# Reordering the opening of a Mamba-2 block that feeds an MLP: where the long row sums, the weights' exponents and their signs are made

## The chip, the cores and the metric

The kernel runs on one core of a Trainium2 chip. The metric is the device time of one execution in microseconds (us). Several runs are taken, and their median counts. One further execution was recorded by the hardware profiler; views of the profile and the trace below are of that execution.

The engines are named as in the profile: PE is TensorE's matrix products, PEld its weight loads, DVE is VectorE, ACT is ScalarE, POOL is GpSimd and SP is SyncE, whose queue issues most of the transfers. A name like L579 is a line of the kernel before the change. The changed kernel's lines lie one to three later.

## The reference

Two parts follow each other. The first is a state-space block over 4 batches, 8 heads and 768 tokens, with head size 32 and state size 16; the second is an MLP over the 3072 tokens, with 256 features in, 2048 inside and 256 out.

```python
log_a = np.log(np.clip(a, 1e-06, 1.0))
for c in range(nc):                       # blocks of tokens
    cum = np.cumsum(la, axis=-1)
    L = np.exp(cum[..., :, None] - cum[..., None, :]) * causal
    M = einsum('bhin,bhjn->bhij', Cc, Bc) * L
    y = einsum('bhij,bhjd->bhid', M, xc) \
        + einsum('bhin,bhnd->bhid', Cc, state) * exp(cum)
    state = exp(sum(la)) * state \
        + sum_j(Bc * xc * exp(cum[..., -1:] - cum))
x = y.transpose(0, 2, 1, 3).reshape(3072, 256)
h = x @ w_in
out = (h * clip(h + 3, 0, 6) / 6) @ w_out
```

All inputs but `w_in` and `w_out` are float32; those two are float64 and come to the kernel as pairs of 32-bit words.

## The kernel before the change

**Blocks.** The 768 tokens of each batch are worked on in six blocks of 128 (halves of 64 inside the block); all four batches and eight heads of a block go together. Block 0 goes through the state-space part first. Then the MLP of block k runs on TensorE while the state-space part of block k + 1 and the preparation of block k + 2 are put between its products by hand. The order of the instructions on each engine is the order of the calls in the program; each engine works its own list in that order and waits by semaphores for the data.

**The opening.** All that the change touches is between the first transfer and the first product of block 0's MLP:

- SyncE issues the loads of `a`, of `C` for block 0 (eight transfers, L101), of `x` (L119) and of the second quarter of `w_in` (L139). ScalarE's queue issues the first quarter of `w_in` and block 0's `B`.
- `log_a` clips `a` and takes the logarithm (L264, L266). `add_up` makes running sums along a row with one VectorE scan (L269), in two pieces: the columns of blocks 0 and 1 (256 wide), and those of blocks 2 to 5 (512 wide). Only the first piece is needed for blocks 0 and 1.
- Blocks 0 and 1 get their decays from products: `diff_mask`, `mask_again`, `diff_less` and `diff_pick` write the differences of the sums into PSUM (L336, L343, L348, L357), and `diff_exp` takes the exponential on ScalarE (L365). Blocks 2 to 5 get theirs from memory: `store_rows` sends the long sums to DRAM (`cum_e`, `cum_d`, L286 and L288) to be loaded again, spread over the partitions; `turn_cum` turns them on TensorE into `c_ps` (L316), and `by_token` copies `c_ps`, negated, into `cum_n` (L319). `cum_n` is used as a bias from block 2 on.
- `turn_b` turns `B` on TensorE (L422) and copies it on ScalarE (L431). `turn_squares` (L465) and `part_heads` (L475) turn `C` on VectorE; `fade` (L481, GpSimd) scales it for the products with the state.
- `scores` forms the products of C and B on TensorE (L530) in four PSUM banks, f0 to f3, and then, in `into_state`, the new states (L548). `multiply` reads the states on ScalarE (L564, L574) and multiplies the scores into the decays on VectorE, one multiply for each of the four banks (L579).
- `mix` forms y from these and x (L625) and from the state (L503), in two halves of the heads; `keep` copies it to SBUF on ScalarE (L639). The first projection (`mlp_in`, L647) begins with that, in 16 units of 128 inner features.
- `busy(n, bank)` puts n idle products into a bank (L493): 128x512 in float32, whose results nobody reads.

**The weights.** A quarter of the float64 words is turned to float32 by `decode(i)`, a generator; each call of `weights(i, n)` runs n steps of it. Quarters 0 to 3 are `w_in`, 4 to 7 are `w_out`. Its steps: a copy of the top 16 bits (ScalarE, L198); the significand (VectorE, L201, L205); exponent and sign masked out (VectorE, L215, L217); the exponent in two steps on ScalarE (L221, L223); sign and exponent joined by a bitwise OR (VectorE, L228) and the product with the significand (VectorE, L236), these two in one step. Three raw buffers are in use, so `load_w` for quarter i + 3 waits until quarter i is read.

The PSUM tiles c_ps (bank f1) and the idle tile (bank f0) are allocated behind `multiply`, which reads the scores from these banks.

Of the kernel before, what the change touches and what calls it, by code (L numbers as in the profile page):

```python
# [8 lines left out]
FP32 = mybir.dt.float32  # L9
# [5 lines left out]
ALU = mybir.AluOpType  # L15
# [6 lines left out]
def kernel(  # L22
# [24 lines left out]
    nc = tc.nc  # L47
    P = 128
    NB, NH, S, D = x.shape
    N = B.shape[-1]  # L50
    DM, DF = moe_w_in.shape[0], moe_w_out.shape[0]
    NC = S // P
# [15 lines left out]
    ps = ctx.enter_context(tc.tile_pool(name="ps", bufs=1, space=PSUM))  # L68
# [7 lines left out]
    G = NB * NH  # L76
# [51 lines left out]
    def load_w(i, queue=nc.sync):  # L128

        raw = loads.tile([P, NK * FP * 2 * P], U32, name="raw", bufs=NRAW)  # L130
        if i < NP:
            cols = slice(2 * i * FP * P, 2 * (i + 1) * FP * P)
            src = moe_w_in[:, cols].rearrange("(k p) f -> p k f", p=P)
            dst = raw.rearrange("p (k f) -> p k f", k=NK)
        else:
            r0 = (i - NP) * FP * P
            src = moe_w_out[r0:r0 + FP * P, :].rearrange("(k p) m -> p k m", p=P)
            dst = raw.rearrange("p (k m) -> p k m", k=FP)
        queue.dma_start(out=dst, in_=src)  # L139
        raws[i] = raw  # L140
# [14 lines left out]
    def conceal_in(t, pattern):  # L155
# [24 lines left out]
        out=head, in_=head, pattern=[[-2 * N, NQ], [-N, 2]], compare_op=ALU.is_ge,  # L180
        fill=0.0, base=0, channel_multiplier=1)
    nc.gpsimd.affine_select(
        out=head, in_=head, pattern=[[2 * N, NQ], [N, 2]], compare_op=ALU.is_ge,
# [3 lines left out]
    def decode(i):  # L187

        n = NK * FP * P
        top = raws[i].bitcast(U16).rearrange("p (n w) -> p n w", w=4)[:, :, 3]
        lo, hi = (raws[i].rearrange("p (n w) -> p n w", w=2)[:, :, w] for w in range(2))
        s = att.tile([P, n], U16, name="ws")
        e = att.tile([P, n], U16, name="we")
        m = att.tile([P, n], U32, name="wm")
        nc.scalar.copy(out=s, in_=top)  # L198

        def significand():  # L200
            nc.vector.tensor_scalar(  # L201
                out=m, in0=hi, scalar1=0xFFFFF, scalar2=0x100000,
                op0=ALU.bitwise_and, op1=ALU.bitwise_or)
            yield
            nc.vector.scalar_tensor_tensor(  # L205
                out=m.bitcast(FP32), in0=lo, scalar=2.0 ** -32, in1=m, op0=ALU.mult,
                op1=ALU.add)
            yield

        parts_m = significand()  # L210
        if i == 0:
            next(parts_m)
            next(parts_m)
        yield
        nc.vector.tensor_scalar(  # L215
            out=e, in0=s, scalar1=0x7FF0, scalar2=None, op0=ALU.bitwise_and)
        nc.vector.tensor_scalar(  # L217
            out=s, in0=s, scalar1=0x8000, scalar2=None, op0=ALU.bitwise_and)
        next(parts_m, None)
        yield  # L220
        nc.scalar.activation(e.bitcast(BF16), e, AF.Relu, bias=bias_hi, scale=-8.0)  # L221
        yield
        nc.scalar.activation(e, e.bitcast(BF16), AF.Relu, bias=bias_lo, scale=-1.0)  # L223
        next(parts_m, None)
        if i and i + NRAW < 2 * NP:
            load_w(i + NRAW)
        yield
        nc.vector.tensor_tensor(out=e, in0=e, in1=s, op=ALU.bitwise_or)  # L228
        m, e = m.bitcast(FP32), e.bitcast(BF16)
        if i < NP:  # L230
            dst = w_in[i]
            m, e = (t.rearrange("p (k f) -> p k f", k=NK) for t in (m, e))
        else:
            dst = w_out[:, (i - NP) * FP:(i - NP + 1) * FP, :]
            m, e = (t.rearrange("p (k f) -> p k f", k=FP) for t in (m, e))
        nc.vector.scalar_tensor_tensor(  # L236
            out=dst, in0=m, scalar=2.0 ** -20, in1=e, op0=ALU.mult, op1=ALU.mult)
# [12 lines left out]
    ends_at = (slice(0, 2 * P), slice(2 * P, S))  # L250
# [17 lines left out]
    def add_up(sl):  # L268
        nc.vector.tensor_tensor_scan(  # L269
            out=cum[:, sl], data0=run.rearrange("g c p -> g (c p)")[:, sl], data1=a_sb[:, sl],  # L270
            initial=0.0, op0=ALU.mult, op1=ALU.add)
# [13 lines left out]
    def store_rows():  # L285
        nc.sync.dma_start(  # L286
            out=cum_e[1:].rearrange("c g p -> g c p"), in_=cum_c[:, 1:])
        nc.sync.dma_start(  # L288
            out=cum_d[2:].rearrange("c a g i -> g (c a) i"),
            in_=cum[:, 2 * P:].rearrange("g (k i) -> g k i", i=HT))  # L290
# [21 lines left out]
    cum_n = const.tile([P, NC, G], FP32, name="cum_n")  # L312

    def turn_cum(c_ps):
        for c in range(2, NC):
            nc.tensor.transpose(out=c_ps[:, c], in_=cum_c[:, c], identity=ident[:G, :G])  # L316

    def by_token(c_ps):
        nc.vector.tensor_scalar(  # L319
            out=cum_n[:, 2:], in0=c_ps[:, 2:], scalar1=-1.0, scalar2=None, op0=ALU.mult)  # L320


    yTs, states, mids, bTs, bss, tmps = {}, {}, {}, {}, {}, {}
# [67 lines left out]
    def ends(c, b):  # L391

        if b == 0:
            bss[c] = att.tile([P, G, N], FP32, name="bs", bufs=1)
        hs = slice(b * NH, b * NH + NH)
        nc.gpsimd.tensor_tensor(  # L396
            out=bss[c][:, hs], in0=Bs[c][:, hs],
            in1=Ls[c][:, b, :, HT - 1:HT].to_broadcast([P, NH, N]), op=ALU.mult)
# [8 lines left out]
    def turned(c):  # L407
        if c not in bTs:
            bTs[c] = [att.tile([P, NB, P], FP32, name="bT", bufs=1),
                      att.tile([P, NB, 2, P], FP32, name="cT", bufs=1),  # L410
                      att.tile([P, NB, P], FP32, name="csT", bufs=1)]
        return bTs[c]

    def turn_ps(c, j):

        if c < 2:
            return ps.tile([P, NB, P], FP32, name="t_ps", tag=f"f{2 * j if c else 1}")
        return ps_o.tile([P, NB, P], FP32, name="t_ps", tag="o")

    def transposes(c, j, t_ps):  # L420
        for b in range(NB):
            nc.tensor.transpose(  # L422
                out=t_ps[:, b],
                in_=bcs[c][j][:, b * NH:(b + 1) * NH].rearrange("s h n -> s (h n)"),
                identity=ident)

    def turn_b(c):

        t_ps = turn_ps(c, 1)
        transposes(c, 1, t_ps)  # L430
        nc.scalar.copy(out=turned(c)[0], in_=t_ps)  # L431
# [47 lines left out]
    def fade(c, sl=slice(0, P), engine=nc.vector):  # L479
        csT = turned(c)[2][:, :, sl]  # L480
        engine.tensor_tensor(out=csT, in0=csT, in1=etos[c][:, :, sl], op=ALU.mult)  # L481
# [8 lines left out]
    def busy(n, bank):  # L490

        for _ in range(n):
            nc.tensor.matmul(  # L493
                out=bank.rearrange("p (b i) -> p b i", b=NB), lhsT=ident,
                rhs=ident.unsqueeze(1).to_broadcast([P, NB, P]), start=True, stop=True)
# [117 lines left out]
    def mix(c):  # L613


        xt = xts[c]
        if (1, 0) not in ys[c]:
            own_halves(c)
        more = c in range(TURN, NC - 1)
        for u in range(2):  # L620
            for b in range(NB):
                for h in range(u * HU, (u + 1) * HU):
                    for a, rows in enumerate(HALF):
                        d0 = D * (h % HU)
                        nc.tensor.matmul(  # L625
                            out=ys[c][a, u][d0:d0 + D, b], lhsT=xt[rows, b * NH + h],
                            rhs=Ls[c][rows, b, h], start=(b == 0 and a >= min(c, 1) and u >= more), stop=True,
                            tile_position=(a * HT, d0), skip_group_check=True)
            if c == 0:
                from_state(c, 1, (2 * u, 2 * u + 1))  # L630
        if c:
            from_state(c, 1)
# [373 lines left out]


    parts = {i: decode(i) for i in range(2 * NP)}

    def weights(i, n):  # L1010
        for _ in range(n):
            next(parts[i], None)


    def diff(c, *bs):
        for part in (diff_less, diff_pick):
            for b in bs:
                part(c, b)
# [16 lines left out]
    first_eto()  # L1035
    diff(1, 2, 3)
    weights(0, 1)
    for b in range(NB):
        ends(0, b)
    turn_b(0)  # L1040
    diff(1, 0, 1)
    weights(0, 1)
    diff_exp(1, 2)
# [1 line left out]
    turn_squares(bcs[0][0], turned(0)[2])  # L1045
    part_heads(0)
    fade(0, HALF[1], nc.gpsimd)
    add_up(ends_at[1])
    store_rows()
    load_w(2)  # L1050
    weights(0, 1)
# [1 line left out]
    scores(0)  # L1053
    multiply(0)
    load_w(3)
    c_ps = ps.tile([P, NC, G], FP32, name="c_ps", tag="f1")
    turn_cum(c_ps)
    busy(1, ps.tile([P, NB * P], FP32, name="d", tag="f0"))
    weights(0, 1)
    weights(1, 1)  # L1060
    by_token(c_ps)
    mix(0)
    keep(0)
    weights(1, 3)
# [180 lines left out]
```

## Time and profile before

| what | value |
|---|---|
| median of 3 runs | 340.89 us (340.2 to 341.09) |
| the profiled execution | 339.78 us, span of its instructions 337.6 us |
| TensorE (PE) busy | 330.6 us |
| VectorE (DVE) busy | 234.5 us |
| ScalarE (ACT) busy | 199.4 us |
| GpSimd (POOL) busy | 123.9 us |
| data moved | 25.15 MB |
| first product of block 0's MLP (L647) | 22.53 us after the start of the span |

The profiled execution took 339.78 us; 2.2 us of that lie outside the span, which runs from the first to the last instruction in the trace. Times in the timeline count from the start of the span. A timeline row gives start, duration, engine, line, operation, what it writes and reads, and in brackets how long the engine was idle before it and what ended that. A row with "x2" or "x4" merges that many instructions, and its duration runs from the first start to the last end. In the chain of waits each row is a link of the chain that ended last: start, length, what. In busy times by stretch, each row is a stretch and the busy time in it of PE, PEld, DVE, ACT and POOL, then the clock that the throttle granted, the busy share of the 16 DMA engines and GB/s.

### The profile page before, as it was taken

What the parts mean: (1) busy time and instruction counts of PE and PEld (TensorE: products, weight loads), DVE (VectorE), ACT (ScalarE), POOL (GpSimd) and SP (SyncE); (2) the same over time, 40 slices, a digit from 0 to 9 for tenths busy, and PEclk for the clock granted to TensorE, in tenths of its full rate; (3) what the DMA queues carried; (4) which work ended last, traced back from release to release, by engine and by line L of the source; (5) the groups of instructions that cost most, each with busy time, mean ns of one, the idle gap of its engine ahead of it and who ended that gap; (6) DMA issues with size and microseconds to landing.
All of it is one profiled execution on the core that took longest, in us unless ns stands there. A gap on an engine that the chain in (4) does not pass through costs nothing.

```text
span 337.6 us, 8192 instructions
## 1 busy us (share of the span) xinstructions
PE 330.6 (98%) x3337; PEld 265.4 (79%) x3337; DVE 234.5 (69%) x380; ACT 199.4 (59%) x418; POOL 123.9 (37%) x123
## 2 busy tenths in 40 slices
PE   6999999999999999999999999999999999999996
PEld 2554448888888888888888888888888888899995
DVE  6699999998399739755339556355477355599974
ACT  4769878757986670576461576570486030577661
POOL 3300000290184799089813079911079800000000
PEclk9999999999999999999999999999999999999999
DMA  8999968042590215258107267101160001110001
GB/s 174 165 316 201 208 219 184 2 54 76 139 142 1 57 37 139 33 72 78 33 13 156 33 83 69 28 4 17 27 81 2 2 2 18 26 21 2 1 2 62
DMA packets 89605, 25.15 MB, mean 75 GB/s; under 512 B 82208, under 2 KB 85952, under 8 KB 89056
## 3 DMA queue, kind: packets, MB, share of 16 engines
q1 hardware_dynamic: 85184, 23.33, 37.5%
q10 hardware_dynamic: 4384, 1.31, 1.8%
q8 instruction: 26, 0.43, 0.5%
q14 instruction: 11, 0.09, 0.1%
HBM read 21.33 MB, written 3.29 MB: 73 GB/s over the span
## 4 chain that ended last, share of the span: by engine, by line
PE 94%; DMA 3%; DVE 1%; SPq 1%; issue 0%; DVEq 0%
PE h L715 33%; PE wb L914 13%; PE wc L914 8%; PE o L772 8%; PE h L647 8%; PE wa L914 8%; PE o_end L880 6%; PE y L625 3%; PE y L503 2%; PE cb L530 2%; DMA raw<-in_moe_w_in_dram 2%; DMA pairs<-in_C_dram 1%; PE y L548 1%; SPq L101 1%; PE o_end L898 1%; PE sp L548 0%
## 5 line engine op out<-in xcount | busy, mean ns | idle before, releaser
L759 DVE SCALAR_TENSOR_TENSOR gT<-gT,h 128x512 f32<-128x512 f32 x96 | 64.8, 684 | 33.8 <-ACT gT L754 32.2
L754 ACT ACTIVATE gT<-h,half 128x512 f32<-128x512 f32 x96 | 65.2, 685 | 25.6 <-PE h L715 23.6
L735 ACT ACTIVATE h<-h 128x512 f32<-128x512 f32 x66 | 38.2, 585 | 39.0 <-PE h L715 38.8
L715 PE MATMUL h<-y_hi,w_part 128*128 128x512 f32 x160 | 51.5, 407 | 0.0
L715 PE MATMUL h<-y_less,w_part 128*128 128x512 f32 x160 | 50.1, 399 | 0.0
L715 PE MATMUL h<-y_lo,w_part 128*128 128x512 f32 x160 | 49.5, 395 | 0.0
L818 POOL TENSOR_TENSOR s<-gT 128x512 f32<-128x512 f32 x16 | 23.8, 1490 | 46.7 <-DVE gT L759 46.7
L715 PEld LDWEIGHTS h<-y_lo,w_part 128*128 128x128 f32 x160 | 30.0, 188 | 7.3
L715 PEld LDWEIGHTS h<-y_hi,w_part 128*128 128x128 f32 x160 | 30.0, 188 | 6.8 <-DVE gT L759 0.2
L715 PEld LDWEIGHTS h<-y_less,w_part 128*128 128x128 f32 x160 | 29.2, 188 | 6.0 <-ACT h L735 0.2
L385 ACT ACTIVATE L<-L,cum_n 128x64 f32<-128x64 f32 x128 | 31.6, 336 | 0.0
L772 PE MATMUL o<-w_out,gT 128*128 128x256 f32 x128 | 28.8, 381 | 0.0
L647 PE MATMUL h<-yT,w_in 128*128 128x512 f32 x64 | 27.7, 594 | 0.0
L772 PEld LDWEIGHTS o<-w_out,gT 128*128 128x128 f32 x128 | 24.1, 190 | 3.8 <-issue 0.5
L647 PEld LDWEIGHTS h<-yT,w_in 128*128 128x128 f32 x64 | 12.1, 190 | 14.9 <-issue 13.2
L158 POOL TENSOR_SCALAR_AFFINE_SELECT L<-L 64x1024 f32<-64x1024 f32 (+1 forms) x16 | 20.4, 1281 | 8.5 <-DMA L<-cum_d 8.0
L579 DVE TENSOR_TENSOR L<-L,cb 128x512 f32<-128x512 f32 x24 | 15.0, 681 | 11.7 <-PE cb L530 11.7
L403 POOL TENSOR_TENSOR tmp<-state,eto 128x256 f32<-128x256 f32 x5 | 3.2, 643 | 52.8 <-ACT eto L389 48.9
L818 POOL TENSOR_TENSOR s<-gT,s 128x512 f32<-128x512 f32 x16 | 21.7, 1364 | 0.9
L396 POOL TENSOR_TENSOR bs<-B,L 128x128 f32<-128x128 f32 x24 | 11.2, 486 | 29.5 <-ACT L L385 20.9
L880 PE MATMUL o_end<-v_pair,g_pair 128*128 128x256 f32 x120 | 21.1, 281 | 0.0
L818 POOL TENSOR_TENSOR gT<-gT 128x512 f32<-128x512 f32 x16 | 20.4, 1279 | 0.9
(140 smaller groups left out, 593.0 us busy)
## 6 DMA issues: line engine op xcount, KB each, us to landing
raw<-in_moe_w_out_dram SPq DMA_DIRECT2D x4, 1024.0 KB
L<-cum_d SPq DMA_DIRECT2D x8, 512.0 KB
xt<-in_x_dram SPq DMA_DIRECT2D x6, 512.0 KB
raw<-in_moe_w_in_dram SPq DMA_DIRECT2D x3, 1024.0 KB
out_dram<-back SPq DMA_DIRECT2D x128, 16.0 KB
pairs<-in_C_dram SPq DMA_DIRECT2D x40, 32.0 KB
eto<-cum_e SPq DMA_DIRECT2D x20, 64.0 KB
B<-in_B_dram SPq DMA_DIRECT2D x5, 256.0 KB
```

Of the source, the lines that this page charges most:

```text
L158: nc.gpsimd.affine_select(out=t[rows], in_=t[rows], pattern=pattern, compare_op=ALU.is_ge, fill=-1e5, base=base, channel_multiplier=-1)
L385: nc.scalar.activation(Ls[c][:, b, h], Ls[c][:, b, h], AF.Exp, bias=cum_n[:, c, g:g + 1])
L579: nc.vector.tensor_tensor(out=Ls[c][:, :, hs], in0=Ls[c][:, :, hs], in1=cbs[c][q], op=ALU.mult)
L647: nc.tensor.matmul(out=h, lhsT=w_in[f // FP][:, j, f % FP * P:(f % FP + 1) * P], rhs=yTs[k][:, j].rearrange("p b i -> p (b i)"), start=(j ...
L715: nc.tensor.matmul(out=hs_[k, f], lhsT=w[j][:, f % FP * P:(f % FP + 1) * P], rhs=y[:, j], start=(start and j == 0), stop=True, skip_group_ ...
L735: nc.scalar.activation(h, h, AF.Copy, scale=1.0 / EPS + 1.0)
L754: nc.scalar.activation(gTs[k][:, f], h, AF.Relu, bias=half, scale=1.0 / 6.0)
L759: nc.vector.scalar_tensor_tensor(out=g, in0=g, scalar=1.0, in1=h, op0=ALU.min, op1=ALU.mult)
L772: nc.tensor.matmul(out=o[:, b % 2], lhsT=gTs[0][:, f, b * P:(b + 1) * P], rhs=w_out[:, f], start=(f == 0 and b % 2 == 0), stop=True, skip_ ...
L818: nc.gpsimd.tensor_tensor(out=o, in0=p_, in1=q_, op=op)
L880: nc.tensor.matmul(out=ends_["cross" if n == 2 else "squares"][b], lhsT=g_parts[t][n][:, b * P:(b + 1) * P], rhs=w, start=(t == 0 and b < ...
L914: nc.tensor.matmul(out=bank[:, slot], lhsT=lhs[:, j], rhs=rhs[:, j], start=(clear and j == 0), stop=True, skip_group_check=True)
```

## The change

Four edits, all in the opening:

1. The long piece of the row sums (`add_up(ends_at[1])`) is made ahead of C's turning on VectorE instead of behind it. With that, `turn_cum` and `by_token` move from behind `multiply` to right behind `turn_b`, `c_ps` takes bank f2 instead of f1, and `store_rows` finds its sums made earlier.
2. `by_token` runs on ScalarE instead of VectorE.
3. One step of `weights(0, 1)` is moved, so that the first exponent step (L221) comes ahead of the copy of the turned B on ScalarE. For quarter 0 `decode` gets one more `yield`, between the OR and the product: the OR runs ahead of `scores` and `multiply`, and the product stays behind them.
4. `busy(1)` ahead of `mix` is left out. `busy(2)` ahead of `scores` stays.

```diff
@@ decode
         yield
         nc.vector.tensor_tensor(out=e, in0=e, in1=s, op=ALU.bitwise_or)
+        if i == 0:
+            yield
         m, e = m.bitcast(FP32), e.bitcast(BF16)
@@ by_token
-        nc.vector.tensor_scalar(
-            out=cum_n[:, 2:], in0=c_ps[:, 2:], scalar1=-1.0, scalar2=None, op0=ALU.mult)
+        nc.scalar.mul(cum_n[:, 2:], c_ps[:, 2:], -1.0)
@@ the opening
     first_eto()
     diff(1, 2, 3)
     weights(0, 1)
+    add_up(ends_at[1])
     for b in range(NB):
         ends(0, b)
+    weights(0, 1)
     turn_b(0)
+    c_ps = ps.tile([P, NC, G], FP32, name="c_ps", tag="f2")
+    turn_cum(c_ps)
+    by_token(c_ps)
     diff(1, 0, 1)
     weights(0, 1)
     diff_exp(1, 2)
     diff_exp(1, 3)
     turn_squares(bcs[0][0], turned(0)[2])
     part_heads(0)
     fade(0, HALF[1], nc.gpsimd)
-    add_up(ends_at[1])
     store_rows()
     load_w(2)
     weights(0, 1)
     busy(2, ps.tile([P, NB * P], FP32, name="d", tag="f3"))
     scores(0)
     multiply(0)
     load_w(3)
-    c_ps = ps.tile([P, NC, G], FP32, name="c_ps", tag="f1")
-    turn_cum(c_ps)
-    busy(1, ps.tile([P, NB * P], FP32, name="d", tag="f0"))
     weights(0, 1)
     weights(1, 1)
-    by_token(c_ps)
     mix(0)
     keep(0)
```

## The prediction

> **What bounds the kernel now.** I read the page first, then the chain of waits from the start to 52 us, then the timeline of the first 24 us engine by engine, then busy time by stretches. From the page:
>
> ```profile
> PE 330.6 (98%) x3337; PEld 265.4 (79%) x3337; DVE 234.5 (69%) x380; ACT 199.4 (59%) x418; POOL 123.9 (37%) x123
> ...
> PE 94%; DMA 3%; DVE 1%; SPq 1%; issue 0%; DVEq 0%
> ```
>
> TensorE is 94% of the chain that ends last; only the opening has other links. The chain there (start us, us, what):
>
> ```profile
> 8.91 4.00 DMA pairs<-in_C_dram
> ...
> 13.09 1.17 DVE csT L465
> ...
> 14.28 0.89 DVE cT L475 x2
> ...
> 15.30 1.25 PE cb L530 x59
> ...
> 16.56 1.30 DVE L L579 x2
> ...
> 17.90 0.43 PE c_ps L316 x4
> 18.33 1.05 PE d L493 x2
> 19.39 1.00 PE y L625 x57
> 20.38 0.61 PE y L503 x16
> 20.99 1.00 PE y L625 x54
> 21.99 0.61 PE y L503 x16
> 22.60 27.66 PE h L647 x64
> ```
>
> The opening waits for C to land (12.91), turns it on VectorE, forms the scores, multiplies them into the decays, and after two of the four multiplies goes to TensorE and stays there. Between the second multiply (17.86) and the mixing (19.39) stand two things that the mixing doesn't use: the turning of the row sums (c_ps, needed only from block 2 on) and two idle passes of `busy(1)`. From 22.60 on TensorE has no gap; the stretch below (busy time of PE, PEld, DVE, ACT, POOL; clock; DMA) stands for those after it up to 330 us, so what the opening saves or loses reaches the end unless a producer falls behind.
>
> ```profile
> 14.60:16.40 1.80, 1.37 (x65) 0.98 (x64) 1.68 (x3) 0.99 (x1) 1.10 (x1) 1.00 0.97 255
> 16.40:17.90 1.50, 0.89 (x71) 0.70 (x65) 1.34 (x3) 0.58 (x3) 0.41 (x1) 1.00 1.05 416
> ...
> 100.00:150.00 50.00, 50.00 (x523) 42.09 (x522) 36.16 (x53) 28.41 (x71) 32.91 (x28) 1.00 0.27 52
> ```
>
> **The change, part by part.**
>
> *Off TensorE's path.* c_ps leaves the place before the mixing (0.43, with 0.04 ahead of it) and the idle passes are gone (1.05). What is late next? The built program shows that the mixing's first product waits for ScalarE and the first multiply, the fifth for the second multiply. The four multiplies take 2.48, so 0.62 each, and end near 17.2, 17.8, 18.4 and 19.0. ScalarE's read of the new state ends at 17.32 + 0.37 = 17.69. So the mixing flows from 17.90, where c_ps started on that same second multiply: 19.39 - 17.90 = 1.49 earlier. Its second half starts 1.61 later, at 19.5, when the fourth multiply is done. It ends near 21.1 instead of 22.6.
>
> *c_ps in its new place*, behind B's turning. There it needs the long row sum (1.21 in row L269). That scan now follows L217, which ends at 10.23; it ends at 11.44 in VectorE's idle wait for C (2.86 before 13.09). TensorE comes to c_ps at 11.74, so it doesn't wait. The four transposes push what follows by 0.36 (17.90 to 18.26, the next start). Cover: TensorE waits 0.43 for cT before the scores. It holds, with 0.07 to spare; without it the scores slip by up to 0.36. I take 0 and keep 0.36.
>
> *ScalarE.* The copy `by_token` has no row there; a 128x128 read of PSUM is 0.63 / 2 = 0.32 (L574), a 128x512 one 0.59 (L431). It replaces 0.28 on VectorE (L319). The first exponent step (1.15) goes ahead of B's copy: it needs L215 (done 9.77), starts at 11.04 behind the opening's Exp, and B's copy moves from 11.95 to about 12.15. ScalarE then does by_token, the second exponent step and two Exps (1.07), and is done near 15.1; before, it was done at 15.60 and idle until 17.32. B's copy is needed at 15.30, the Exps at 16.43 (they free the banks of the new state). Cost 0; even at 0.59 it stays hidden, and below zero it can't go, since nobody waits there now.
>
> *VectorE.* The scan's place behind cT is taken by the signs' OR (0.68, row L228): 15.15 to 15.8, while TensorE forms scores until 16.5. Its exponents are there by 14.1. Behind the multiplies only the last product of the weights is left (1.22), so the first quarter of w_in is ready at about 20.2, against 20.89; TensorE needs it at 21.1. VectorE goes on to the second quarter at 20.1 instead of 21.02, 0.92 earlier; its idle 0.54 before the next OR (wait for ScalarE) is then used up, which makes it 1.46 earlier.
>
> ```profile
> 18.75 1.15 ACT L198 COPY ws<-raw 128x1024 uint16<-128x1024 uint16 x1 [0.53 <-DMA raw<-in_moe_w_in_dram]
> ...
> 25.28 0.69 DVE L228 TENSOR_TENSOR we<-we,ws 128x1024 uint16<-128x1024 uint16 x1 [0.54 <-ACT we L223]
> ...
> 48.12 1.23 DVE L236 SCALAR_TENSOR_TENSOR w_out<-wm,we 128x1024 f32<-128x1024 f32 x1
> ```
>
> *Who can fall behind.* In the first projection (16 units of 1.73 from 22.60) the last quarter of w_in is ready at 42.33 and used at 43.35; the first of w_out is ready at 49.35 (row above) and used at 50.27. The slacks are 1.02 and 0.92. With VectorE only 0.92 earlier they are 0.44 and 0.34: no stall at either bound.
>
> *SyncE.* Row sums leave earlier: the queue is free at 13.92 (L139: 10.43 + 3.49) and waited until 16.31 for the scan. Now cum_e, cum_d and the third quarter of w_in go out from about 14.0, the latter at 14.8 instead of 17.17. Nobody waits for these earlier; whom they may delay is the second rival.
>
> Sum: -1.49 (-1.13 with the transposes uncovered). In the profiled execution (339.78; span 337.6) that gives 338.3. The median of the three runs is 340.89, 1.1 above that execution, and the runs spread from 340.2 to 341.09. So I forecast 340.89 - 1.49 = 339.4, give or take 0.6.
>
> **Rivals.**
>
> *1. The clock falls (slower).* The same 128x512 bf16 pass takes 631 ns up to 6.4 us and 379 ns from 7.5 on, with PEclk at 1.00 all the time: TensorE starts at half pace and gets up to pace only after 4.9 to 5.4 us of work from 2.13 on, and that column doesn't show it. Now the longest stretch without a full-array pass is 14.87 to 18.26, 3.4 us; after the change it is from about 15.2 to 21.1, 5.9 us, of small tiles with 0.7 of idle time. If small tiles count as rest, and a rest between 3.4 and 5.9 us is enough, the first projection starts at half pace and loses half of 4.9 to 5.4, some 2.6: 340.89 - 1.49 + 2.6 = 342.0. Against it: after the 3.4 us the passes of `busy(1)` took 592 ns, as before them, and TensorE's real gaps stay below 0.7. [...] No row here tells what counts as busy. Chance 0.09.
>
> *2. The weights' second quarter lands later.* The third quarter now joins the queue 2.4 us earlier, while the second is under way (landed 18.75, row L198). If the two share the engines, the second is up to 2.4 late; ScalarE's copy (1.15) and the four copies behind it (0.37 each) then end at 21.4 plus the delay, while TensorE wants the last of them at 21.1 + 0.86 = 21.96. Beyond 0.6 each further us is lost: at worst 1.8, so 341.2. Against it: x stood before the second quarter in that queue and was there at 16.43, and the rate then rose from 255 to 416 GB/s, so one transfer mostly follows the other. [...] Chance 0.07, most of it within 0.3%.
>
> *3. VectorE becomes the bound.* It is busy 25.97 of 27.7 us in the first projection. If it gained nothing, TensorE would wait 1.49 - 0.92 = 0.57 for w_out: 340.0. For it: hardly any idle time; against: the 1.22 + 0.28 taken off it and the idle 0.54. Chance 0.06.
>
> **How the numbers follow.** 0.3% (1.0 us) is about what can be told from no change. Forecast 0.74, rivals 0.09, 0.07 and 0.06, 0.04 for something else. Faster: 0.70 (the forecast, less 0.04 for a gain that scatter makes too small). Same: 0.04 + rival 3 + 0.05 of rival 2 + 0.02 = 0.17. Slower: 0.09 + 0.02 + 0.02 = 0.13. The range goes from 339.4 less 0.7 to 340.7, which takes in the uncovered transposes, rival 3 and half of rival 2.
>
> **What would show it.** Right: the long scan ends before 11.5, c_ps starts near 11.75, the scores still at 15.30, on the chain the multiply is followed at once by the mixing, at 17.9, and the first projection starts at 21.1 with passes of 592 ns. Wrong: passes above that at 21 to 26 us (rival 1); the copy at L198 starting after 19.3 (rival 2); the output products waiting for L236 near 49 (rival 3); scores later than 15.4 (the transposes uncovered).

## The result and the profile after

The changed kernel takes 344.11 us (median of 6 runs, 342.68 to 346.14), the kernel before 340.51 in runs on the same chip (6 runs, 339.65 to 341.09). The ratio is 1.0112, 95% interval [1.0078, 1.0146]: slower by 3.6 us, where 1.5 us of gain was forecast. The profiled execution took 343.91 us with a span of 341.8.

The page of the changed kernel, busy time and granted clock by fortieths of the span:

```profile
PE 332.1 (97%) x3335; PEld 266.4 (78%) x3335; DVE 234.4 (69%) x379; ACT 199.7 (58%) x419; POOL 123.4 (36%) x123
...
PEclk9987999999999999999999999999999999999999
...
q8 instruction: 26, 0.43, 0.5%
```

TensorE does two products less (the idle passes) and is busy 1.5 us longer; its clock dips in the third and fourth slice (17 to 34 us). Queue 8 will be needed below: 26 packets, 0.43 MB. The chain of waits of the changed kernel through the opening:

```profile
12.08 0.36 PE c_ps L318 x4
...
15.52 1.21 PE cb L531 x54
16.73 0.80 PE y L549 x53
17.56 0.38 ACT adds L565
17.94 0.04 issue
17.98 0.89 PE y L626 x51
18.87 2.59 issue
21.46 0.31 PE y L626 x6
21.77 0.61 PE y L504 x16
22.39 0.83 PE y L626 x53
23.22 1.04 PE y L504 x16
24.26 30.44 PE h L648 x64
```

The mixing starts at 17.98, as forecast, and flows for 0.89 us. Then TensorE stands still for 2.59 us with the releaser "issue": no engine, semaphore or transfer in the trace lets it go. The first projection starts at 24.26 instead of 22.60 (+1.66) and takes 30.44 instead of 27.66 (+2.78). Together that is 4.4, about the 4.2 between the two spans. Busy time by stretch (PE, PEld, DVE, ACT, POOL; clock; DMA) shows both halves of the loss:

```profile
17.90:21.46 3.56, 0.89 (x58) 0.73 (x58) 3.10 (x6) 1.67 (x4) 0.00 (x0) 1.00 1.05 397
22.99:29.82 6.83, 6.83 (x42) 3.47 (x26) 4.06 (x7) 4.64 (x6) 0.00 (x0) 0.50 0.92 295
100.00:150.00 50.00, 50.00 (x524) 42.15 (x523) 37.65 (x54) 28.70 (x71) 32.99 (x27) 1.00 0.37 60
```

In the first, TensorE works 0.89 of 3.56 us while the transfers run at 397 GB/s. In the second it works all the time at a granted clock of 0.50, which costs 6.83 x 0.5 = 3.4 us (0.6 at the end of the mixing, 2.78 in the projection); from 29.82 on it is back at 1.00, and the stretch from 100 to 150 us is as before.

The timeline of the changed kernel, the rows that answer to steps of the forecast:

```profile
10.31 1.21 DVE L271 TENSOR_TENSOR_SCAN pre<-pre 32x512 f32<-32x512 f32 x1
...
12.60 0.29 ACT L321 ACTIVATE cum_n<-c_ps 128x128 f32<-128x128 f32 x1
...
15.09 0.69 DVE L228 TENSOR_TENSOR we<-we,ws 128x1024 uint16<-128x1024 uint16 x1
...
14.64 0.39 SPq L288 DMA_DIRECT2D cum_e<-pre  x1
...
15.55 1.65 SPq L139 DMA_DIRECT2D raw<-in_moe_w_in_dram  x2
...
19.69 1.11 ACT L198 COPY ws<-raw 128x1024 uint16<-128x1024 uint16 x1 [1.23 <-DMA raw<-in_moe_w_in_dram]
...
26.94 0.69 DVE L228 TENSOR_TENSOR we<-we,ws 128x1024 uint16<-128x1024 uint16 x1 [2.37 <-ACT we L223]
```

The scan, by_token and the OR are where they were put, beside other work. SyncE's stores leave at 14.64 instead of 16.31, and the second quarter of the weights is there at 19.69 instead of 18.75.

### The profile page after: what moved, and what is told of

It reads as the page before. It is cut to its first block, busy times and chain, and to the rows that moved or that the text cites. A ratio compares the mean times of both kernels' runs of the same rounds, so it can differ in the third digit from the quotient of the medians.

```text
span 341.8 us, 8191 instructions
## 1 busy us (share of the span) xinstructions
PE 332.1 (97%) x3335; PEld 266.4 (78%) x3335; DVE 234.4 (69%) x379; ACT 199.7 (58%) x419; POOL 123.4 (36%) x123
## 4 chain that ended last, share of the span: by engine, by line
PE 96%; DVE 1%; DMA 1%; issue 1%; ACT 0%
PE h L716 33%; PE wb L915 12%; PE h L648 9%; PE wc L915 8%; PE o L773 8%; PE wa L915 8%; PE o_end L881 6%; PE y L626 3%; PE y L504 2%; PE cb L531 2%; DMA pre<-in_a_dram 1%; PE y L549 1%; PE d L358 1%; PE d L349 1%; PE d L494 1%
## 5 line engine op out<-in xcount | busy, mean ns | idle before, releaser
L648 PE MATMUL h<-yT,w_in 128*128 128x512 f32 x64 | 30.5, 641 | 0.0
L648 PEld LDWEIGHTS h<-yT,w_in 128*128 128x128 f32 x64 | 13.2, 208 | 16.6 <-issue 14.6
L881 PE MATMUL o_end<-v_pair,g_pair 128*128 128x256 f32 x120 | 21.1, 281 | 0.0
L819 POOL TENSOR_TENSOR gT<-gT 128x512 f32<-128x512 f32 x16 | 20.4, 1281 | 0.9
```

The lines of the kernel that those rows point to most:

```text
L648: nc.tensor.matmul(out=h, lhsT=w_in[f // FP][:, j, f % FP * P:(f % FP + 1) * P], rhs=yTs[k][:, j].rearrange("p b i -> p (b i)"), start=(j ...
L819: nc.gpsimd.tensor_tensor(out=o, in0=p_, in1=q_, op=op)
L881: nc.tensor.matmul(out=ends_["cross" if n == 2 else "squares"][b], lhsT=g_parts[t][n][:, b * P:(b + 1) * P], rhs=w, start=(t == 0 and b < ...
```

## The experiments

**First question: what holds TensorE, and does leaving out the idle passes suffice for it?** Only `busy(1)` is taken out of the kernel before, or put back into the changed one.

```diff
 e1 (kernel before)                    e2 (changed kernel)
-    busy(1, ... tag="f0"))           +    busy(1, ... tag="f0"))
```

> The kernel before with only the idle passes ahead of the mixing (busy(1)) left out; row sums, signs and exponents stay where they were. Theory I (instruction supply): TensorE's next block of instructions is fetched as before (packet near 17.8, usable near 20.1), and the mixing now reaches the end of the block it has at about 19.3, so TensorE pauses about 0.8 us inside the mixing, the first projection starts near 22.3 and the clock stays: 340 to 341 us, within 0.3% of before. Theory S (small tiles alone lower the clock, the pause is not needed for it): no full-array pass from 14.9 to 21.5, the granted clock falls to 0.50 for about 6.8 us, and the time is some 2 us above before, 342 to 343. My original forecast, carried over: 1.05 less, 339.5.

> The changed kernel with busy(1) back ahead of the mixing. Theory I: the instruction packet still moves near 19.2 and is usable near 21.4, so the mixing still pauses, but only about 1.6 us, and the first projection starts near 24.2, as in the changed kernel; if a shorter pause and one full-array burst keep the clock at 1.00 the time is about 342 (1.6 above before), else it is as slow as the changed kernel, 344. Theory S: with the full-array passes back the clock stays, there is no pause to speak of, and the time is 340.5 or less (the 0.43 of the row sums gained).

e1: 343.67 us, ratio 1.0089 [1.0053, 1.0126]. e2: 344.43, ratio 1.0108 [1.0079, 1.0138]. Their chains of waits, e1 first:

```profile
18.41 0.74 PE y L625 x50
19.15 1.76 issue
...
23.87 30.24 PE h L647 x64
```

```profile
18.68 0.83 PE y L626 x50
19.51 2.18 issue
...
24.58 30.33 PE h L648 x64
```

Taking the idle passes out is enough for a pause (1.76) and a lower clock (0.990 over the execution, the projection takes 30.24). The two came together, so e1 doesn't tell the two theories apart, and the pause was twice what was expected. Putting the passes back cures neither, though two full-array passes then end at 18.68. So their absence isn't the only cause: something else in the change makes the pause as well.

**Second question: where does the pause come?** Eight tiny products, read by nobody, go in front of `mask_again`, far ahead of the mixing.

```diff
+    for _ in range(8):
+        nc.tensor.matmul(
+            out=ds[0, 0][:32, 0, :8], lhsT=ident_h[:, :32], rhs=hide[:, :8], start=True, stop=True)
     for b in range(3):
         mask_again(0, b)
```

> The changed kernel with 8 tiny products (8 weight loads and 8 products of 8 columns) more on TensorE ahead of mask_again, where TensorE waits anyway; a mark for where the pause falls. Theory I: the pause comes 8 products earlier in the mixing, after 50 recorded products of it instead of 58 (the block of instructions ends at a fixed count). If the pause is a wait for data (a bank, a multiply, a copy), it stays behind the 58th. Time about as the changed kernel, 343 to 346.

343.77 us, ratio 1.0087 [1.0055, 1.0119]. Its timeline:

```profile
17.80 0.82 PE L626 MATMUL y<-L,xt 64*32 64x64 f32 x50 [0.46 <-ACT adds L565]
21.39 0.34 PE L626 MATMUL y<-L,xt 64*32 64x64 f32 x14 [2.76 <-issue]
```

The changed kernel stops after 58 products of the mixing, this one after 58 - 8 = 50, and e2, with two passes more ahead of it, after 56. In every run with a pause it stands behind the 349th or 350th recorded product, a fixed place in TensorE's list of instructions, whatever these are. 3335 products and as many weight loads make 6670 instructions; over the 26 packets of q8 instruction that is 257 for each, and 0.43 MB / 26 = 16 KB. From this I take the packets of queue 8 for TensorE's instructions, and the pause for a wait at the border of such a block; no row names what the packets hold or which engine they are for. In the changed kernel the border costs 2.59 us in the open.

DMA by queue (packets, MB, share), in the tenth of a microsecond in which the block for the mixing moves: the kernel before at 17.8, the changed kernel at 19.2.

```profile
q8 instruction: 1, 0.02, 62.4%
```

```profile
q8 instruction: 1, 0.02, 59.6%
```

In the changed kernel TensorE goes on 2.2 us behind the packet (19.28 to 21.46); in all runs with a pause it was 2.2 to 2.6. For the kernel before this puts the block in place at 20.0 to 20.4. By the count (e7 and e8, with the same list of products, stop after 57 of the mixing) it is wanted at about 20.0; the row of the kernel before for the window 19.3 to 20.03:

```profile
19.32 0.90 PE L625 MATMUL y<-L,xt 64*32 64x64 f32 x57
```

The 58th product starts at 20.07 in that trace. By this estimate the block arrives just in time, and the trace names no wait there. Of 29 executions of the kernel before taken beside e13 to e15, two took 342.42 and 343.06 us at a clock of 0.995; whether the block came too late in these was not recorded.

When the block is asked for is not in the trace. By an estimate it is not late: 257 instructions are 128 products, so counted in recorded products the borders would lie 128 apart (93, 221, 349 and on), and 16 of the 26 packets in the trace of the kernel before move when TensorE is less than 30 products short of such a place. If a block is asked for when TensorE comes to the block ahead of it, the one for the mixing is asked for behind product 221, at 16.2 in the kernel before and 16.4 in the changed one. From there to the packet it is 1.6 and 2.9 us.

**Third question: what makes the packet late?** The suspects were the requests that now leave SyncE earlier. e3: the changed kernel with the third quarter asked for at 18.63. e8: the kernel before with the long scan early, so that its stores leave at 14.84 and the third quarter's request at 15.75; all else stays.

```diff
 e3 (changed kernel; also gated by a one-column write to the raw tile)
-    load_w(2)
     multiply(0)
+    load_w(2, gate=True)
 e8 (kernel before)
+    add_up(ends_at[1])
     for b in range(NB):
         ends(0, b)
...
-    add_up(ends_at[1])
     store_rows()
```

> The changed kernel with the third quarter of w_in requested only when ScalarE has read the new states (near 18.4 instead of 15.5; one copy of a single column more on ScalarE). Theory I with DMA load: with less in the queues the instruction packet moves near 17.8 again and the pause shrinks from 2.6 to about 1.2, the first projection starts near 22.7; the clock may or may not fall; 340.5 to 342. Theory I without DMA load (the packet is late because it is asked for late): pause and time stay as in the changed kernel, 344. Theory S: clock falls all the same, 342 or more.

> The kernel before with only the long row sum made ahead of C's turning, so that its stores and the third quarter of w_in leave 1.7 us earlier; c_ps, signs, exponents and busy(1) stay where they were. My forecast's working: no change, 340.6. Theory I2: the stores delay the second quarter of w_in to 19.4 or later, the instruction packet with it to about 19.2, usable at 21.5; the mixing needs it at 20.3, so it pauses about 1.2 us with busy(1) in place; if the clock then falls, 343; if so short a pause leaves it, 341.8.

e3: 344.21 us, ratio 1.011 [1.0082, 1.0139]; the packet moves at 19.3, as in the changed kernel, and the pause is 2.64. The third quarter is not the cause. e8: 342.07 us, ratio 1.0044 [1.0022, 1.0065]; the packet moves at 19.5 and the chain shows the pause in a kernel that still has `busy(1)` and everything else of before:

```profile
19.62 0.83 PE y L625 x50
20.46 1.40 issue
21.86 0.31 PE y L625 x7
...
24.20 29.29 PE h L647 x64
```

One scan moved ahead on VectorE, and nothing on TensorE, is enough. How much later the packet gets by it is less sure, as its time scatters: in e1, with the requests of the kernel before, it moved at 18.66. e8's ten runs fall into two groups: five at a granted clock of 0.999 or 1.000 took 340.83 to 341.45 us (middle value 340.98, 0.4 above the kernel before), five at 0.994 or 0.995 took 342.69 to 343.35, another 2.1. The trace with the pause of 1.40 is of the second group; how long the first group paused is not recorded.

**Fourth question: does the packet follow the second quarter?** In e5 and e6 (the changed kernel, without and with `busy(1)`) the second quarter is asked for at 15.27 and 15.06, with the third and fourth right behind; in e7 (the kernel before) at 14.43. e9 asks for it in four pieces of 32 partitions. e10 asks for it only behind ScalarE's read of the new state, at 18.06.

```diff
 e5, e6, e7, e10 (gate: a one-column write to the raw tile by ScalarE)
-    load_w(1)
...
+    load_w(1, gate=True)      # e5, e6, e7: behind fade(); e10: behind take(0), with load_w(2)
...
-    weights(1, 1)
     mix(0)
     keep(0)
+    weights(1, 1)
 e9
-        queue.dma_start(out=dst, in_=src)
+        for rows in [slice(32 * r, 32 * r + 32) for r in range(4)] if i == 1 else [slice(0, P)]:
+            queue.dma_start(out=dst[rows], in_=src[rows])
```

> The changed kernel, with the second quarter of w_in requested behind the opening's last Exp (near 15.3 instead of 10.4; one copy of a single column on ScalarE makes it wait) and its exponent copy moved behind the four copies of y, so that it doesn't hold them. Nothing else is changed. Theory I2 (the instruction packet waits in the DMA engines behind that 1 MB transfer, since in all runs it moved 0.3 to 0.9 us before the transfer was complete): the packet moves by 16.5, is usable before the mixing needs it at 18.9, there is no pause, and the first projection starts near 21.3. With the pause gone the clock then tells on small tiles: if it stays at 1.00, a pause is what lowered it, and the time is 1.2 to 1.5 below before, 339.2; if it falls to 0.50 between 19 and 24 us (theory S), some 342. If the packet is late because TensorE asks late (theory I1), packet near 19, pause and clock as in the changed kernel, 344.

> As the run before, with busy(1) back ahead of the mixing. Theory I2: no pause, the clock stays under either view of small tiles, the first projection starts near 22.3, and the time is 0.3 to 0.5 below before, 340.1. Theory I1: 344.

> The kernel before with only the second quarter of w_in requested behind the Exp (near 15.7) and its exponent copy moved behind the copies of y. Theory I2: the instruction packet, which came just in time before (usable near 20.1, needed at 20.2), comes 1.5 us or more earlier; nothing waited for it in the profiled execution, so the time stays within 0.3% of before, 340.6, with less scatter. Theory I1: packet near 17.8 as before, same time.

> The changed kernel with the second quarter of w_in loaded by four transfers of 32 partitions, 256 KB each, in the place of one. Theory I2 in the form that an instruction packet waits for the whole of what an engine has taken on from one transfer: it now waits for a quarter only, moves near 17 and is usable near 19.3, so the pause is 0.5 us or less; then about 340, and about 342 if the clock falls all the same. If the queue order of bytes is what counts, packet near 19.2, pause 2.6 and 344 as in the changed kernel.

> The changed kernel with the second and third quarters of w_in requested only when ScalarE has read the first new state (near 17.8), after the instruction block is asked for (near 16). Theory I2: with nothing but x and the stores in the queues the packet moves by 17, usable by 19.3, pause below 0.5 us, mixing done by 21.6. The second quarter then lands near 22, and the fifth unit of the first projection waits about 1 us for it, so no gain is expected from this version. It tells the clock's cause: windows without a full-array pass but without a long pause. Clock at 1.00: 340 to 341. Clock at 0.50 with the pause gone: small tiles suffice, 342 to 344. Theory I1 (asked for late): packet near 19.2 and pause as in the changed kernel.

| run | us | ratio, interval | packet at | pause |
|---|---|---|---|---|
| e5 | 345.46 | 1.0138 [1.0117, 1.016] | 20.4 | 4.00 |
| e6 | 344.82 | 1.012 [1.0091, 1.0149] | 20.0 | 2.74 |
| e7 | 344.35 | 1.0119 [1.0084, 1.0153] | 19.1 | 1.24 |
| e9 | 345.0 | 1.0147 [1.0123, 1.0171] | 20.5 | 4.28 |
| e10 | 342.3 | 1.0064 [1.0048, 1.0081] | 17.4 | 0.95 |

Four are misses: a somewhat later or cut request pushes the packet back further. e10 is the one that asks for the weights after the packet, and there it moves at 17.4, the earliest of all, though TensorE runs as in the changed kernel until it stops (18.88 against 18.87). It missed as well, in size: a pause below 0.5 and 340 to 341 us were expected. Its timeline:

```profile
19.83 0.31 PE L630 MATMUL y<-L,xt 64*32 64x64 f32 x6 [0.95 <-issue]
...
22.08 7.13 PE L652 MATMUL h<-yT,w_in 128*128 128x512 f32 x16
```

Even then 0.95 us of pause stay: from product 221 (16.37) TensorE needs 2.5 us for the 128 products to the border, and the next block is in use only 3.5 us after that point. The projection starts at 22.08, 0.45 before the kernel before (22.53), but the weights land too late (copy at 23.55), VectorE falls behind with them, and the time is 2.1 us worse (340.21 for the kernel before on that chip).

**Fifth question: is it a line?** e11 puts the stores behind the third quarter in the changed kernel, e12 adds `busy(1)`. My expectation was that the stores were in the packet's way.

```diff
-    store_rows()
     load_w(2)
+    store_rows()
```

> The changed kernel, with the two stores of the row sums issued behind the request for the third quarter of the weights and so queued behind the second and third quarter; everything else stays. Theory (the early stores push the second quarter, and with it the block of TensorE's instructions): the packet of queue 8 moves near 17.85 us as in the kernel before instead of 19.25, the block can be used near 20.1 to 20.3, the mixing starts at 17.98 and stops after 58 products for 1.2 to 1.4 us instead of 2.59, and the first projection starts near 22.0. If the clock then stays at 1.00, the time is 339.8 to 340.2 (340.5 for the kernel before); if a pause of that size is still enough to lower the clock, the projection takes some 2.8 longer and the time is 342.5 to 343. Rival (the packet is late for another reason, such as TensorE reaching the end of its block earlier): the packet stays near 19.2, the pause near 2.6, the time near 344.

> As the run before it, with the idle product busy(1) put back ahead of the mixing, so that only the row sums, their transposes and the operations on other engines are earlier than in the kernel before. Theory: the packet moves near 17.9, the mixing starts near 19.0, TensorE wants the next block after 56 products near 19.9 and has it near 20.1 to 20.3, so the pause is 0.2 to 0.5, the first projection starts near 21.9 to 22.1, the clock stays at 1.00 and the time is 339.8 to 340.2. Rival (the packet is late for another reason): packet near 19.2, pause near 2.2, clock at 0.50 for some us, time near 344.4 as when the idle product alone was put back.

e11: 345.65 us, ratio 1.0148 [1.0129, 1.0168]; e12: 344.93, ratio 1.0128 [1.0111, 1.0145]. Both theories missed: the second quarter lands earlier (copy at 19.18 against 19.69) and the packet still moves later, at 20.1 to 20.2, with pauses of 3.85 and 3.08. The chain of e11:

```profile
17.71 0.89 PE y L626 x51
18.60 3.85 issue
22.45 0.43 PE y L626 x6
```

The single packets in the traces show what had started by then. A quarter is 256 packets of 4 KB. In the kernel before 247 of them have started when the block moves, in the changed kernel all 256, 7 of the third quarter and more than half of the stores' packets. In e11 and e12, with the third quarter right behind the second, some 430 have started: nearly two quarters. In e10 it is none. So in these traces the block moves when most of what was asked for ahead of it on the loads' queue has started.

e13 to e15 test that: of the second quarter only the first half (128 packets) is asked for early; the second half, the stores and the third quarter follow the first scores (e13, and e15 in the kernel before) or the first new states (e14).

```diff
-    load_w(1)
+    load_w(1, part=0)
...
-    store_rows()
-    load_w(2)
...
     scores(0)
+    load_w(1, part=1, gate=cbs[0][0][:, 0, 0, :1])     # e14: behind take(0), and weights(1, 1) behind keep(0)
+    store_rows()
+    load_w(2)
     multiply(0)
```

> The changed kernel, with the second quarter of the weights asked for in two halves: the first where the quarter stood, the second, then the two stores, then the third quarter behind the first bank of scores (ScalarE writes one column of the raw tile from it, so the requests leave near 17.0 us). Theory (the block of instructions waits behind whatever was asked for before it): behind half a quarter the packet moves near 17.4 as it did with nothing in line, the block can be used near 19.8, the pause in the mixing is near 1.0 instead of 2.59, the clock stays at 1.00, the first projection starts at 22.1 to 22.2 with 592 ns passes, the second half lands by 19.9, and the time is 340.0 to 340.4, some 0.2 to 0.5 below the kernel before. If the requests of 17.0 still get ahead of the packet, it moves near 18.5 to 20, the pause is 2 to 3 and the time 343 to 344.5. Rival (the line has nothing to do with it): packet near 19.2 whatever is in line, time near 344.

> As e13, but the second half, the stores and the third quarter are asked for behind ScalarE's read of the first new state, near 18.1 us, and the quarter's exponents are copied behind the mixing's results. Theory: packet near 17.4, pause near 1.0, clock 1.00, first projection at 22.1; the second half lands near 20.7, its copy starts at 22.6 instead of 23.55 in the run with the whole quarter late, so the weights of the second quarter are there near 29.3, where TensorE wants them near 29.2: time 340.1 to 340.6. Rival: packet near 19.2, time near 344.

> The kernel before with e13's order of requests and nothing else changed. Theory: its block is there before it is wanted either way (packet 17.4 instead of 17.85, wanted near 20.2), so there is no pause, the mixing starts near 19.4, the first projection near 22.6 and the time is 340.3 to 340.8, the same as before; e13's gain over it, 0.2 to 0.5, is then the changed kernel's own. Rival (the order of requests itself gains or loses): a time away from 340.5 by more than 0.5.

| run | us | ratio, interval | packet at | 4 KB packets ahead | pause |
|---|---|---|---|---|---|
| e13 | 342.45 | 1.0053 [1.0029, 1.0077] | 18.8 | 166 | 2.35 |
| e14 | 342.09 | 1.0038 [1.0017, 1.0059] | 17.6 | 122 | 1.18 |
| e15 | 340.65 | 0.9994 [0.9978, 1.0011] | 17.6 | 121 | none |

In e14 and e15 the block moves when the half in line is nearly through; in e13 the second half got ahead of it, the worse of the two cases named. e15 takes as long as the kernel before, but the order of requests is not free there: the projection starts at 23.25 instead of 22.53, as ScalarE copies the quarter's exponents, once the later half is there (21.53 to 22.65), ahead of the mixing's results. What makes up for these 0.7 us was not found. e14's timeline:

```profile
19.89 0.31 PE L634 MATMUL y<-L,xt 64*32 64x64 f32 x6 [1.18 <-issue]
...
22.14 7.13 PE L656 MATMUL h<-yT,w_in 128*128 128x512 f32 x16
29.92 14.14 PE L656 MATMUL h<-yT,w_in 128*128 128x512 f32 x32 [0.65 <-DVE gT L768]
44.42 7.13 PE L656 MATMUL h<-yT,w_in 128*128 128x512 f32 x16 [0.36 <-DVE w_in L242]
```

The projection starts 0.39 earlier than before (22.53) and loses it again to VectorE, which has the later weights to work off, so the expected 340.1 to 340.6 us were missed. Five of its twelve runs kept a clock of 1.000 and took 340.76 to 341.74; five at 0.990 took 342.5 to 343.11. No order of requests tried gave a version that beats the kernel before. A variant of e13 with `busy(1)` was not run: with its block as early as in e15 it could save the 0.43 of c_ps at best, which is below what a measurement here can tell.

**The clock.** In the changed kernel its falls and rises lie a multiple of 3.41 us apart (17.07 at 1.00 up to the fall at 22.99, then 6.83 at 0.50, 314.03 at 1.00), and in the kernel before the one stretch at 1.00 is 331.09 long, 97 times 3.41. Stretches of that length, the changed kernel, then e8, then e10:

```profile
16.17:19.58 3.41, 2.24 (x159) 1.75 (x146) 2.79 (x5) 0.90 (x3) 0.19 (x1) 1.00 0.92 334
19.58:22.99 3.41, 1.52 (x86) 1.37 (x86) 2.92 (x5) 1.86 (x3) 0.00 (x0) 1.00 1.02 413
22.99:26.40 3.41, 3.41 (x38) 2.12 (x22) 1.55 (x4) 2.43 (x4) 0.00 (x0) 0.50 0.81 304
```

```profile
20.63:24.04 3.41, 2.18 (x103) 1.93 (x103) 3.34 (x7) 1.37 (x4) 0.00 (x0) 1.00 1.02 418
24.04:27.45 3.41, 3.41 (x10) 1.52 (x6) 1.48 (x4) 2.56 (x3) 0.00 (x0) 0.50 0.79 245
```

```profile
18.40:21.81 3.41, 2.46 (x143) 2.05 (x125) 2.01 (x3) 1.16 (x4) 0.00 (x0) 1.00 0.78 228
21.81:25.22 3.41, 3.41 (x20) 1.66 (x17) 0.49 (x2) 1.67 (x4) 0.00 (x0) 1.00 1.02 411
```

Stretches with 2.24 and 2.46 us of TensorE work are followed by clock 1.00, stretches with 1.52 and 2.18 by 0.50. But busy time does not sort them. Two stretches of e5 in a row, then one of e10 whose next is at 1.00 as well (clock 0.999 over that execution):

```profile
16.55:19.97 3.42, 1.88 (x134) 1.43 (x122) 3.16 (x5) 0.90 (x3) 0.00 (x0) 1.00 0.89 315
19.97:23.38 3.41, 0.49 (x14) 0.40 (x16) 0.45 (x1) 0.14 (x1) 0.00 (x0) 1.00 1.02 413
```

```profile
28.62:32.03 3.41, 1.68 (x5) 0.61 (x4) 3.34 (x6) 1.81 (x4) 0.00 (x0) 1.00 0.92 304
```

1.88 us of small products and 1.68 us of full-array products were followed by 1.00, 2.18 us of small products in e8 were not. A count of what fills the array does better. Let a product count its columns times the part of the 128x128 array that it fills: 512 for a full 128x512 pass, 16 for one of the scores, 8 for one of the mixing's products. Cut in steps of 3.41 us, up to 336 us, the traces of the kernel before and the changed one hold 189 stretches at clock 1.00 that are followed by 1.00; they count 1430 (at 16.17 in the changed kernel, small tiles with 0.7 us of pause) to 7613. The one that is followed by 0.50 (19.58) counts 630. In the rows above, e8's 103 products make at most 824, followed by 0.50, and e10's 143 at most 1144, followed by 1.00. The measure was chosen after the fact, and what the chip itself goes by is not shown. That a pause falls into one such stretch in some executions and is shared by two in others would fit the two groups of times of e8 and e14; this is a guess, as one execution of each was traced.

## Why the prediction was wrong, point by point

- **The step that failed** is in the first part of the sum: "So the mixing flows from 17.90 ... It ends near 21.1 instead of 22.6." The start was right within 0.08 us (17.98), though behind ScalarE's read of the new state (done 17.94, put at 17.69) and not the second multiply. The flow was not right: it took for granted that TensorE's next instruction is always there. c_ps and the idle passes covered what these runs point to as a wait for a block of instructions; the 1.49 us taken away came back as pause, and with a later block as 2.59.
- **The second failure** is "Nobody waits for these earlier", on SyncE's requests. The scan made early, and with it these requests, bring the pause into the kernel before (e8). They are not in the packet's way by themselves, as e11 showed; with them the packets of the second quarter run late (the 128th starts at 17.6 instead of 16.6), and the block's with them. How the early stores slow a transfer that stands ahead of them is not shown.
- **Rival 1** had the right side, nearly the right price and half of the mechanism. It gave 342.0 for a clock at half pace; 344.1 was measured, as the pause came on top and the clock cost 3.4 (2.78 in the projection) instead of 2.6. With 0.95 us of pause among small tiles the clock stayed at 1.00 in the profiled execution of e10 (two of its four executions show 0.995 and 0.990). It fell in the changed kernel with 2.59 us of pause and in e8 with 1.40; in e2, with 2.18 us of pause behind two full-array passes, the mean over the execution is 0.990. That the PEclk column doesn't show a half clock held for the passes of 631 ns in the first 6.4 us, but not here, where it shows 0.50.
- **Rival 2** asked the right thing of the wrong queue. Its sign came true: the copy at L198 started at 19.69, behind 19.3. ScalarE's copies hid it in the pause; the waiting party was TensorE, for 2.59 us in which no engine and no transfer is named. And it named the third quarter, which e3 cleared.
- **Rival 3** didn't come up in the changed kernel, where no product of the first projection waits for VectorE; e14 shows it once the pause is short, with 0.65 + 0.36 us of TensorE waiting for VectorE.
- **Right** were the terms off TensorE's path: the scan ends at 11.52 (11.44 forecast), c_ps starts at 12.01 (11.74); by_token takes 0.29 (0.32); the OR runs 15.09 to 15.78 (15.15 to 15.8); the first quarter of w_in is ready at 20.41 (20.2). One small sign of being wrong came true: the scores start at 15.45, later than 15.4, as TensorE comes to them from its idle passes (done 15.52) and no longer waits for cT. The transposes were no longer covered in full; but `a` also landed later in this execution (the first clip at 4.16 instead of 3.99), so how much of the 0.15 is theirs is not shown.

## What to carry to other kernels

A wait that no row shows can end just in time behind idle-looking work: before idle passes or side work are taken off a busy engine, count its instructions and look at the packets that seem to bring them (here one at 17.84, and the first product behind the border at 20.07). Stretches of small products came to such a border fastest (58 in 0.89 us), and a bulk load asked for just before them moved the packet back here, from 17.4 with none in line to 20.1 with two quarters. A pause among small products was followed by a clock of 0.50 in the changed kernel, and that cost more (3.4 us) than the pause (2.59). A request moved ahead because "nobody waits" can still go with a later packet (17.84 in the kernel before, 19.5 in e8); look at what else has to come through, instruction packets among them.

## What the runs showed of the hardware that was not expected

- The 26 instruction packets on queue 8 have 16 KB each. In the runs with a pause TensorE went on 2.2 to 2.6 us behind such a packet, and the pause was 0.95 (e10) to 4.28 us (e9), where the small products (58 of them in 0.89 us) reached the border early.
- In these traces such a packet moves when most of the bytes ahead of it on the loads' queue have started: at 17.4 with none in line (e10), 17.6 with half a megabyte (e14, e15), 17.8 to 19.5 with one in a single piece (the kernel before, the changed kernel, e1, e3, e8), 20.1 to 20.2 with two (e11, e12). How the transfers of the two queues take turns is not in the trace.
- The granted clock was 0.50 for 3.41 us in e8 (24.04 to 27.45) and for 6.83 us in the changed kernel (22.99 to 29.82), each behind a stretch of 3.41 us that used little of the array: a count of at most 824 and of 630, where one full 128x512 pass counts 512. Behind 1.23 us of idle time among small products (e8) it was 0.50, and behind 1.73 us among full-array products (e10, 28.62 to 32.03) it was 1.00. In e8 the executions with the lower clock took 2.1 us longer than the others.
